# Attention maxima tiles, stack loads and the change of halves in a fused attention and feed-forward kernel

## Chip, cores and metric

One Trainium2 chip, one of its cores. The metric is device time in microseconds (us) of one execution, the median of several runs; less is better. The kernel before takes 1902.88 us (median of 3 runs, 1902.23 to 1906.19).

The engines of a core are named as in the profile: PE (matmul) with PEld (its weight loads), DVE (vector), ACT (scalar), POOL (GpSimd) and SP, which here issues every DMA. SPq, ACTq, POOLq and DVEq are the sequencers of these engines.

## What is computed

2048 tokens of 576 numbers, in float32. The output is a gated mix of an attention with memory over four quarters of 512 tokens (32 heads of 18) and of a feed-forward part of width 4608:

```
g = sigmoid((x * gate_w).sum(-1))
for each quarter s:                       # q, k, v = x @ wq, x @ wk, x @ wv, by heads
    a_dot = softmax(q k^T * scale + mask) v
    a_mem = phi(q) M / (phi(q) z + 1e-6)
    o     = sig(beta) * a_mem + (1 - sig(beta)) * a_dot
    M, z  = M + phi(k)^T v, z + sum phi(k)
a = concat(o) @ wo
b = (silu(x @ w_gate) * (x @ w_up)) @ w_down
out = g * a + (1 - g) * b
```

## The kernel before

**Numbers in parts.** Float32 products are made of high and low parts (`split`, L106: ACT makes the high part, DVE subtracts it). Attention's q and k are kept as three bf16 parts in DRAM (`stk`, "the stacks"), v likewise in `vd`.

**First part, projections** (to about 223 us): for each quarter nine chains of q and k products (`qk`, L301), then eight v steps n = 0 to 7 (`v_step`, L327) with the memory's output (`mem_step`, L397), which writes tiles `om` that SP stores to `med` in the order of the list `late`. In the last quarter the v steps also hold the first weight splits (`w_make`, L215), memsets of the `kst` tiles (L557) and the loads of the first two attention units' stacks (L559).

**Second part, feed-forward and attention together** (about 223 to 1780 us): two halves of the tokens (quarters 2 and 3, then 0 and 1), each with 36 tiles f of the feed-forward width. A tile f has seven product groups (`seven`, L921) from seven combinations of x (`XO`) and seven operands of weights: in the first half made from raw weights and stored to `wc` and `rc` (`keep`, L240), in the second half fetched from there (`w_fetch`, L586). Operand buffers number six. After each group comes a tick (k = 0 to 7, L958), whose `beat` (L866) runs what `defer` has put down for this tick, then at every third f also down groups (`down_group`, L768, PE L778, added up by DVE L783), and steps of attention by a credit. `defer(o + 1, fn)` puts fn on tick o from now. Instructions stand on each engine in the order in which this code emits them.

**Attention** runs in 64 units u of two heads, five steps n = 0 to 4 each (`att_gen`, L709, step number tau = 5u + n). A step makes score blocks for the row maxima (`s_bank`, L608: PE L615, then DVE L622, which writes a scrap tile `scr` and a column of `mb`), and twelve steps later the score blocks again with the maxima as rows added (`t_bank`, L649: PE L655, exponential on ACT L659, mask on POOL L667). After step n = 1, `m_tr` (L626) turns a unit's maxima, which go through DRAM (`mxd`) into rows of the stack tile (`row_load`, L186). The tiles `mb`, two of them, are allocated and set to zero at L604 and L605, after the pools of the first part are closed. The exponentials are split in two (DVE L732, POOL L734) and multiplied with v (L684, L686). Four stack tiles `qst` and `kst` take turns; `stack_load` (L171) loads one unit in ten DMAs, six for the first head and what both share, four for the second; in `att_gen` at L719 unit u + 1 is loaded at steps n = 2 and 3 of unit u. The score blocks of the first head are made at n = 0, those of the second at n = 1.

**Change of halves.** In the last tile of the first half (f = 35) `x_second` (L885) puts down the work on the new x: per z = 0, 1 four raw loads (L892), four sums on POOL (L897), four splits (ACT L107, DVE L108), three loads of kept operands `xd` (L906), and two of `xsd`. After f = 35 come ten beats (`BREAK`, L1018) with the last sixteen down groups, two in a beat from the third beat on.

**DMA order.** All DMAs are issued by SP in the order of the code. They use eight semaphores in turn, and in the built program each waits until the DMA eight before it has landed.

**Last part** (1780 us on): output product, gate and stores.

The functions that the diff touches, and what calls them:

Of the kernel before, what the change touches and what calls it, by code (L numbers as in the profile page):

```python
# [12 lines left out]
F32 = mybir.dt.float32  # L13
# [7 lines left out]
P = 128  # L21
# [3 lines left out]
DH = 18  # L25
L = 512
NSEG = 4
FT = 36
# [8 lines left out]
NB = 8 * NSEG  # L37
# [9 lines left out]
BREAK = 10  # L47
SLOT = (0, 3, 2, 1, 4, 6, 5)
KR = 6 * DH
# [7 lines left out]
def gated_mix(ctx, tc, xT, wf, wd, wv, wo, beta, cmask, ident, bmask, out):  # L57
    nc = tc.nc
# [109 lines left out]
    ast = ExitStack()  # L168
    VP, accs, cur, unit, ms, mts, mbs = {}, {}, {}, {}, {}, {}, []

    def stack_load(u, pr):  # L171
        s, b = divmod(u, 16)
        q, k = (stk[kind, s, 2 * b * DH:2 * b * DH + 2 * DH].rearrange("(j r) z n -> r j z n", r=DH)
                for kind in range(2))
        tq, tk = qst[u % NST], kst[u % NST]
        for z, n in ((0, 3), (1, 2)):
            r0 = (0, 3 * DH)[z]
            qz = q[:, pr, z]
            nc.sync.dma_start(tq[r0:r0 + n * DH, pr],
                              bass.AP(tensor=qz.tensor, offset=qz.offset, ap=[[0, n]] + list(qz.ap)))  # L180
            nc.sync.dma_start(tk[r0:r0 + n * DH, pr], k[:, pr, 0:n].rearrange("r z n -> z r n"))
        if pr == 0:
            nc.sync.dma_start(tq[5 * DH:KR], q[:, :, 2])
            nc.sync.dma_start(tk[5 * DH:KR], k[:, :, 0])

    def row_load(u):  # L186
        nc.sync.dma_start(qst[u % NST][KR:KR + 3].rearrange("z j (i n) -> z (j i) n", n=P), mxd[u])
# [73 lines left out]
    with ExitStack() as st:  # L261
# [228 lines left out]
        for s in range(NSEG):  # L490
# [32 lines left out]
            if s == 3:  # L523
                qst_.close()
                rp = pool(ctx, "rp", 4, side="right")
                wop = pool(ctx, "wop", 6, side="right")
                kq = pool(ast, "kq", 1, side="right")
                for i in range(NST):
                    qst.append(kq.tile([P, 2, L], BF, name=f"qst{i}"))
                    kst.append(kq.tile([P, 2, L], BF, name=f"kst{i}"))  # L530
                for z in range(2):
                    for j, b, kt in ((0, 2, z), (3, 2, 2 + z), (5, 3, 2 + z)):
                        XO[j][z] = xs_of[b][0][kt]
                wraw_of[0] = [w_load(0, u) for u in range(2)]
                start = w_make(0)
            for n in range(8):
                hf, i = divmod(n, 4)
                flush()
                v_step(s, hf, i)
                if s:  # L540
                    mem_step(s, n // 2, n % 2)
                if s < 2 and n > 1 and n - 2 in ((0, 1, 2, 3), (2, 3))[s]:
                    late.append((xd[s, n - 2], f32(xs_of[s][0][n - 2]).rearrange("p a b -> p (a b)")))
                if s < 2 and n == 6:
                    late.append((xsd[s], f32(xs_of[s][1])))
                if s < 3:
                    if n == 0:
                        xs_of[s + 1] = x_tiles(s + 1)
                    if 1 <= n < 6:
                        x_split(xs_of[s + 1], n - 1, raws["x", n - 1])  # L550
                else:
                    if n == 4:
                        wraw_of[1] = [w_load(1, u) for u in range(2)]
                    if n < 2:
                        first_sum(6, n)
                    elif n < 6:
                        nc.gpsimd.memset(kst[n - 2], -1.0)  # L557
                    if n > 3:
                        stack_load(n // 2 - 2, n % 2)  # L559
                    for _ in range((0, 0, 2, 3, 3, 3, 3, 3)[n]):  # L560
                        if start[0][0] < 8:
                            start.pop(0)[1]()
# [7 lines left out]
    with ExitStack() as st:  # L570
# [15 lines left out]
        def w_fetch(f):  # L586
            ops, rem = [None] * 7, [None] * 2
            wops[1, f], wrem[1, f] = ops, rem

            def one(j):  # L590
                ops[j] = op_tile()
                nc.sync.dma_start(f32(ops[j]).rearrange("p a k n -> p (a k n)"), wc[f, j])

            def two(z):
                rem[z] = rem_tile()
                nc.sync.dma_start(f32(rem[z]).rearrange("p a n -> p (a n)"), rc[f, z])

            late = BREAK if f == 0 else 0
            return [(j + 2 + late * (j == 6), lambda j=j: one(j)) for j in range(7)] + [(4, lambda: two(0)), (8, lambda: two(1))]

        kp = pool(ast, "kp", 2, side="right")
        ap = pool(ast, "ap", 2, side="right")
        for i in range(2):
            mbs.append(kp.tile([P, P], F32, name=f"mb{i}", bufs=1))  # L604
            nc.gpsimd.memset(mbs[i], 0.0)  # L605
        SPLAN = [[(0, 0, 3)], [(0, 1, 3)], [(384, 0, 0), (0, 0, 2)], [(384, 1, 0), (0, 1, 2)], [(0, 0, 1), (256, 1, 1)]]

        def s_bank(u, n):  # L608
# [100 lines left out]
        def att_gen():  # L709
            N = 10 * NB  # L710
            for tau in range(N + TL + VL + 4):
# [4 lines left out]
                    nc.sync.dma_start(mxd[u - 1].rearrange("z q n -> q z n"), mts.pop(u - 1))  # L716
                if n == 0 and 2 <= u <= 2 * NB + 1:
                    row_load(u - 2)
                if n in (2, 3) and 0 < u < 2 * NB - 1:  # L719
                    stack_load(u + 1, n - 2)  # L720
                z = tau - TL - VL - 1
                if z % 20 == 0 and 0 <= z < N and z // 20 + 1 < 4 * NSEG:
                    v_fetch(z // 20 + 1)
# [130 lines left out]
        att = att_gen()  # L854
        hs, ds = {}, {}
        seq = [(half, f) for half in range(2) for f in range(FT)]
        v_fetch(0)
        groups = []
        credit = [-1.0]
        yas = {}  # L860
# [24 lines left out]
        def x_second(new, xs):  # L885
# [6 lines left out]
                nc.sync.dma_start(r[z, q], xT[HALF[1][b], :, kt])  # L892

            def total(z, j):
                c, d, e, g = (r[z, q] for q in range(4))
                o, p, q = {1: (c, d, c), 4: (d, g, d), 2: (g, g, c), 6: (e, e, g)}[j]
                nc.gpsimd.tensor_sub(o, p, q)  # L897

# [10 lines left out]
                xs[b] = xs_tile()  # L909
                nc.sync.dma_start(f32(xs[b]), xsd[b])  # L910

            for z, loads, sums, splits in ((0, (0, 1, 5, 4), (6, 6, 7, 7), (8, 8, 9, 10)),
                                           (1, (9, 9, 11, 10), (12, 12, 13, 13), (13, 14, 14, 15))):
                todo += [(o, lambda z=z, q=q: load(z, q)) for o, q in zip(loads, range(4))]
                for o, p, j in zip(sums, splits, (1, 4, 2, 6)):
                    todo += [(o, lambda z=z, j=j: total(z, j)), (p, lambda z=z, j=j: parts(z, j))]
                todo += [(o + z, lambda z=z, j=j: kept(z, j)) for o, j in ((2, 0), (6, 3), (8, 5))]
            todo += [(11 + b, lambda b=b: rest(b)) for b in range(2)]
            return sorted(todo, key=lambda t: t[0])

        def seven(t, w, x, first, last):  # L921
# [15 lines left out]
        for pos, (half, f) in enumerate(seq):  # L937
# [7 lines left out]
            if nxt:  # L945
                plan += w_make(nxt[1]) if nxt[0] == 0 else w_fetch(nxt[1])
                if half == 0 and f + 2 < FT:
                    wraw_of[f + 2] = [None, None]
                    for u in range(2):
                        plan.append(((2, 5)[u], lambda u=u, f=f: wraw_of[f + 2].__setitem__(u, w_load(f + 2, u))))  # L950
            if pos == FT - 1:
                X2, XS2 = [[None, None] for _ in range(7)], [None, None]
                plan += x_second(X2, XS2)
            for o, fn in plan:
                defer(o + 1, fn)
            step = [0]
# [1 line left out]
            def tick():  # L958
# [3 lines left out]
                    while stores:  # L962
                        nc.sync.dma_start(*stores.pop(0))
                if half == 0:
                    if (q, k) in ((0, 0), (1, 3), (2, 1)):
                        draw[f] = d_load(f)
                    if (q, k) in ((1, 0), (1, 7), (2, 5)):
                        g = f - 1 if k == 0 else f
                        ds[half, g] = d_split(g, draw.pop(g))
                elif (q, k) in ((1, 0), (1, 2), (2, 1)):  # L970
                    g = f - 1 if k == 0 else f
                    ds[half, g] = d_fetch(g)
# [141 lines left out]
```

## Time and profile before

| | |
|---|---|
| median of 3 runs | 1902.88 us (1902.23 to 1906.19) |
| the profiled execution | 1903.28 us, of this its span 1901.6 us |
| mean granted PE clock | 0.991 |
| PE busy | 1820.7 us, 96% of the span |
| DVE, ACT, POOL busy | 1217.8, 958.1, 856.6 us |
| DMA | 337.66 MB, mean 178 GB/s, queue busy 53.7% |

How to read the profile: times are us from the start of the span unless marked ns. A row of a group or a timeline has start, duration, engine, line of the kernel, operation, tiles (out<-in) and, in brackets, how long the engine stood idle just before and what ended that. The wait table adds such waits up. The chain of waits is followed back from the last instruction to what released each step; a DMA in it has its time from issue to landing. Tables by stage give the busy time of each engine in a stretch of the span, the granted PE clock (1.00 is full speed) and the share and rate of the DMA engines.

### The profile page before, as it was taken

What the parts mean: (1) busy time and instruction counts of PE and PEld (TensorE: products, weight loads), DVE (VectorE), ACT (ScalarE), POOL (GpSimd) and SP (SyncE); (2) the same over time, 40 slices, a digit from 0 to 9 for tenths busy, and PEclk for the clock granted to TensorE, in tenths of its full rate; (3) what the DMA queues carried; (4) which work ended last, traced back from release to release, by engine and by line L of the source; (5) the groups of instructions that cost most, each with busy time, mean ns of one, the idle gap of its engine ahead of it and who ended that gap; (6) DMA issues with size and microseconds to landing.
All of it is one profiled execution on the core that took longest, in us unless ns stands there. A gap on an engine that the chain in (4) does not pass through costs nothing.

```text
span 1901.6 us, 36530 instructions
## 1 busy us (share of the span) xinstructions
PE 1820.7 (96%) x12508; PEld 1543.4 (81%) x12508; DVE 1217.8 (64%) x3026; ACT 958.1 (50%) x1778; POOL 856.6 (45%) x1246
## 2 busy tenths in 40 slices
PE   8999979999999999999997999999999999999999
PEld 7889857877877887887786788788878878888899
DVE  5555656777777777777775656565565656655455
ACT  7666444466456546645653544543543454354311
POOL 3324522555545555564555445454444444444121
PEclk9999989999999999999998999999999999999999
DMA  6544384466466456645657644654554464445544
GB/s 236 195 170 167 140 303 159 157 228 208 129 214 228 152 170 231 208 151 193 215 165 255 211 139 134 198 154 120 174 172 122 140 196 147 133 154 155 190 150 138
DMA packets 206474, 337.66 MB, mean 178 GB/s; under 512 B 38416, under 2 KB 95888, under 8 KB 206288
## 3 DMA queue, kind: packets, MB, share of 16 engines
q1 hardware_dynamic: 206288, 335.32, 53.7%
q8 instruction: 100, 1.64, 0.3%
q14 instruction: 86, 0.70, 0.1%
HBM read 197.48 MB, written 137.76 MB: 176 GB/s over the span
## 4 chain that ended last, share of the span: by engine, by line
PE 76%; DVE 7%; DMA 6%; ACT 5%; issue 3%; SPq 1%; POOL 1%; ACTq 0%; DVEq 0%; POOLq 0%
PE bank L925 25%; PE bank L778 23%; PE bank L130 11%; PE bank L931 5%; PE bank L655 3%; PE bank L615 3%; PE bank L684 2%; DMA raw<-in_wf_dram 1%; PE bank L686 1%; ACT L659 1%; DMA woraw<-in_wo_dram 1%; DMA draw<-in_wd_dram 1%; PE bank L362 1%; ACT hh L107 1%; ACT pe L659 1%
## 5 line engine op out<-in xcount | busy, mean ns | idle before, releaser
L734 POOL TENSOR_TENSOR p<-pe,p 128x512 f16<-128x512 f32 x320 | 374.4, 1170 | 684.7 <-DVE p L732 595.1
L778 PE MATMUL bank<-dw,hh 128*128 128x288 f32 x2304 | 482.7, 302 | 21.4 <-DVE ya L783 9.7
L778 PEld LDWEIGHTS bank<-dw,hh 128*128 128x128 f32 x2304 | 379.4, 189 | 43.7 <-DVE ya L783 17.0
L659 ACT ACTIVATE pe<-bank 128x512 f32<-128x512 f32 x320 | 191.2, 598 | 346.0 <-PE bank L655 285.4
L778 PE MATMUL bank<-dw,hl 128*128 128x288 f32 x1152 | 341.1, 296 | 2.0 <-DVE hl L108 2.0
L783 DVE TENSOR_TENSOR ya<-bank,ya 128x288 f32<-128x288 f32 x352 | 160.2, 456 | 232.7 <-PE bank L778 230.7
L622 DVE CUSTOM_DVE_ANT_0 scr<-bank,cm 128x512 bf16<-128x512 f32 (+3 forms) x512 | 247.2, 483 | 15.9 <-PE bank L615 9.1
L778 PEld LDWEIGHTS bank<-dw,hl 128*128 128x128 f32 x1152 | 217.6, 189 | 2.6 <-DVE hl L108 2.6
L655 PE MATMUL bank<-qst,kst 111*128 111x512 bf16 (+3 forms) x512 | 151.7, 305 | 0.7 <-DMA qst<-mxd 0.7
L732 DVE CAST p<-pe 128x512 f16<-128x512 f32 x320 | 150.8, 472 | 0.3 <-POOL pe L667 0.3
L667 POOL TENSOR_SCALAR_AFFINE_SELECT pe<-pe 128x256 f32<-128x256 f32 (+1 forms) x320 | 135.4, 423 | 14.0 <-ACT pe L659 12.8
L615 PE MATMUL bank<-kst,qst 108*128 108x512 bf16 (+3 forms) x512 | 126.3, 300 | 13.2 <-ACT pe L659 12.2
L1006 DVE TENSOR_TENSOR bank<-bank,row 128x512 f32<-128x512 f32 x72 | 50.3, 699 | 110.3 <-ACT row L1002 109.7
L659 ACT ACT_TABLE_LOAD x66 | 84.7, 1283 | 49.2 <-PE bank L655 48.2
L993 ACT ACTIVATE row<-bank 128x512 f32<-128x512 f32 x72 | 43.1, 598 | 127.4 <-PE bank L931 127.0
L108 DVE TENSOR_TENSOR hl<-row,hh 128x512 fp32r<-128x512 f32 x72 | 51.9, 721 | 85.6 <-ACT hh L107 85.6
L130 PE MATMUL bank<-xo,qhi 128*128 128x512 f32 x288 | 92.8, 403 | 5.1 <-ACT xo L107 5.0
L655 PEld LDWEIGHTS <-kst 111*128 111x128 bf16 x512 | 47.9, 97 | 52.3 <-issue 36.9
L997 ACT ACTIVATE bank<-bank 128x512 f32<-128x512 f32 x72 | 41.9, 582 | 90.7 <-PE bank L925 86.8
L999 ACT ACT_TABLE_LOAD x67 | 86.0, 1283 | 1.2
L318 POOL TENSOR_TENSOR q<-qr,q 128x512 bf16<-128x512 f32 x36 | 43.8, 1217 | 93.6 <-ACT q L317 86.9
L982 ACT ACTIVATE bank<-bank 128x512 f32<-128x512 f32 x72 | 42.0, 583 | 82.0 <-PE bank L925 72.0
(2085 smaller groups left out, 4238.1 us busy)
## 6 DMA issues: line engine op xcount, KB each, us to landing
raw<-in_wf_dram SPq DMA_DIRECT2D x72, 320.0 KB
dc<-dw SPq DMA_DIRECT2D x36, 576.0 KB
dw<-dc SPq DMA_DIRECT2D x36, 576.0 KB
stk<-q SPq DMA_DIRECT2D x32, 384.0 KB
draw<-in_wd_dram SPq DMA_DIRECT2D x36, 288.0 KB
vd<-vps SPq DMA_DIRECT2D x8, 912.0 KB
v<-vd SPq DMA_DIRECT2D x16, 456.0 KB
qst<-stk SPq DMA_DIRECT2D x128, 54.0 KB
```

Source lines behind the costliest of these rows:

```text
L130: nc.tensor.matmul(t, st[n], mv[n], start=(n == 0), stop=(n == 13))
L615: nc.tensor.matmul(t[:, c:c + w], qs[:KR, pr, P * i:P * i + P], ks[:KR, pr, 0:w], start=True, stop=True)
L622: nc.vector.tensor_tensor_reduce(scr[:, :w], t[:, c:c + w], cm[:, L - w:L], 1.0, -3.0e38, OP.add, OP.max, m[:, k:k + 1])
L655: nc.tensor.matmul(t[:, c:c + w], ks[:KR + 3, pr, P * j:P * j + P], qs[:KR + 3, pr, P * j:L], start=True, stop=True)
L659: nc.scalar.activation(pe, t, AF.Exp, scale=SCALE)
L667: nc.gpsimd.affine_select(d, d, pattern=pat, compare_op=OP.is_ge, fill=0.0, base=0, channel_multiplier=-1)
L732: nc.vector.tensor_copy(p1, pe)
L734: nc.gpsimd.tensor_sub(p2, pe, p1)
L778: nc.tensor.matmul(t, p, q[:, cs], start=(n == 0), stop=(n == 3 * CH - 1))
L783: nc.vector.tensor_add(ya[:, i, cs], t, ya[:, i, cs])
L925: nc.tensor.matmul(t, w[:, p, z], x[z][:, q], start=first and n == 0, stop=last and n == 5, skip_group_check=True)
L931: nc.tensor.matmul(t, w[:, p], xs, start=False, stop=p == 1, skip_group_check=True)
```

## The change

- `mb` is allocated with the stack tiles and set to zero by POOL in the v steps n = 6 and 7 of the last quarter. What was allocated behind it in `kp` (`scr` and others) moves to its place.
- `stack_load` becomes `stack_loads`, a list of the same ten DMAs. In the v steps only unit 0 is loaded, two DMAs a step from n = 3 on. In `att_gen` unit u + 1 is loaded from u = 0 on in three, three and four DMAs at steps n = 2, 3 and 4.
- The first load of v, `v_fetch(0)`, is put down for the sixth beat.
- `x_second` is put down one tile earlier with 8 more ticks, so that ticks may be negative: the first two raw loads go to ticks -3 and -2 of f = 35, sums, splits, kept operands and `xsd` to other ticks.
- `w_fetch(0)` of the second half: operands 0 to 5 five ticks later, the remainders six; operand 6 stays.
- In the first half `d_load` of every third f moves from k = 0 to k = 3.

```diff
--- before.py
+++ after.py
@@ -168,20 +168,22 @@
     ast = ExitStack()
     VP, accs, cur, unit, ms, mts, mbs = {}, {}, {}, {}, {}, {}, []
 
-    def stack_load(u, pr):
+    def stack_loads(u):
         s, b = divmod(u, 16)
         q, k = (stk[kind, s, 2 * b * DH:2 * b * DH + 2 * DH].rearrange("(j r) z n -> r j z n", r=DH)
                 for kind in range(2))
         tq, tk = qst[u % NST], kst[u % NST]
-        for z, n in ((0, 3), (1, 2)):
-            r0 = (0, 3 * DH)[z]
-            qz = q[:, pr, z]
-            nc.sync.dma_start(tq[r0:r0 + n * DH, pr],
-                              bass.AP(tensor=qz.tensor, offset=qz.offset, ap=[[0, n]] + list(qz.ap)))
-            nc.sync.dma_start(tk[r0:r0 + n * DH, pr], k[:, pr, 0:n].rearrange("r z n -> z r n"))
-        if pr == 0:
-            nc.sync.dma_start(tq[5 * DH:KR], q[:, :, 2])
-            nc.sync.dma_start(tk[5 * DH:KR], k[:, :, 0])
+        r = []
+        for pr in range(2):
+            for z, n in ((0, 3), (1, 2)):
+                r0 = (0, 3 * DH)[z]
+                qz = q[:, pr, z]
+                r += [(tq[r0:r0 + n * DH, pr],
+                       bass.AP(tensor=qz.tensor, offset=qz.offset, ap=[[0, n]] + list(qz.ap))),
+                      (tk[r0:r0 + n * DH, pr], k[:, pr, 0:n].rearrange("r z n -> z r n"))]
+            if pr == 0:
+                r += [(tq[5 * DH:KR], q[:, :, 2]), (tk[5 * DH:KR], k[:, :, 0])]
+        return r
 
     def row_load(u):
         nc.sync.dma_start(qst[u % NST][KR:KR + 3].rearrange("z j (i n) -> z (j i) n", n=P), mxd[u])
@@ -528,6 +530,8 @@
                 for i in range(NST):
                     qst.append(kq.tile([P, 2, L], BF, name=f"qst{i}"))
                     kst.append(kq.tile([P, 2, L], BF, name=f"kst{i}"))
+                for i in range(2):
+                    mbs.append(kq.tile([P, P], F32, name=f"mb{i}"))
                 for z in range(2):
                     for j, b, kt in ((0, 2, z), (3, 2, 2 + z), (5, 3, 2 + z)):
                         XO[j][z] = xs_of[b][0][kt]
@@ -555,8 +559,11 @@
                         first_sum(6, n)
                     elif n < 6:
                         nc.gpsimd.memset(kst[n - 2], -1.0)
-                    if n > 3:
-                        stack_load(n // 2 - 2, n % 2)
+                    else:
+                        nc.gpsimd.memset(mbs[n - 6], 0.0)
+                    if n > 2:
+                        for z in stack_loads(0)[2 * n - 6:2 * n - 4]:
+                            nc.sync.dma_start(*z)
                     for _ in range((0, 0, 2, 3, 3, 3, 3, 3)[n]):
                         if start[0][0] < 8:
                             start.pop(0)[1]()
@@ -595,14 +602,11 @@
                 rem[z] = rem_tile()
                 nc.sync.dma_start(f32(rem[z]).rearrange("p a n -> p (a n)"), rc[f, z])
 
-            late = BREAK if f == 0 else 0
-            return [(j + 2 + late * (j == 6), lambda j=j: one(j)) for j in range(7)] + [(4, lambda: two(0)), (8, lambda: two(1))]
+            late = [5 * (1 + (j == 6)) * (f == 0) for j in range(7)]
+            return [(j + 2 + late[j], lambda j=j: one(j)) for j in range(7)] + [(4 + 6 * (f == 0) + 4 * z, lambda z=z: two(z)) for z in range(2)]
 
         kp = pool(ast, "kp", 2, side="right")
         ap = pool(ast, "ap", 2, side="right")
-        for i in range(2):
-            mbs.append(kp.tile([P, P], F32, name=f"mb{i}", bufs=1))
-            nc.gpsimd.memset(mbs[i], 0.0)
         SPLAN = [[(0, 0, 3)], [(0, 1, 3)], [(384, 0, 0), (0, 0, 2)], [(384, 1, 0), (0, 1, 2)], [(0, 0, 1), (256, 1, 1)]]
 
         def s_bank(u, n):
@@ -716,8 +720,9 @@
                     nc.sync.dma_start(mxd[u - 1].rearrange("z q n -> q z n"), mts.pop(u - 1))
                 if n == 0 and 2 <= u <= 2 * NB + 1:
                     row_load(u - 2)
-                if n in (2, 3) and 0 < u < 2 * NB - 1:
-                    stack_load(u + 1, n - 2)
+                if n > 1 and u + 1 < 2 * NB:
+                    for d in stack_loads(u + 1)[(0, 3, 6)[n - 2]:(3, 6, 10)[n - 2]]:
+                        nc.sync.dma_start(*d)
                 z = tau - TL - VL - 1
                 if z % 20 == 0 and 0 <= z < N and z // 20 + 1 < 4 * NSEG:
                     v_fetch(z // 20 + 1)
@@ -854,7 +859,7 @@
         att = att_gen()
         hs, ds = {}, {}
         seq = [(half, f) for half in range(2) for f in range(FT)]
-        v_fetch(0)
+        defer(6, lambda: v_fetch(0))
         groups = []
         credit = [-1.0]
         yas = {}
@@ -892,7 +897,7 @@
                 nc.sync.dma_start(r[z, q], xT[HALF[1][b], :, kt])
 
             def total(z, j):
-                c, d, e, g = (r[z, q] for q in range(4))
+                c, d, e, g = (r.get((z, q)) for q in range(4))
                 o, p, q = {1: (c, d, c), 4: (d, g, d), 2: (g, g, c), 6: (e, e, g)}[j]
                 nc.gpsimd.tensor_sub(o, p, q)
 
@@ -909,13 +914,13 @@
                 xs[b] = xs_tile()
                 nc.sync.dma_start(f32(xs[b]), xsd[b])
 
-            for z, loads, sums, splits in ((0, (0, 1, 5, 4), (6, 6, 7, 7), (8, 8, 9, 10)),
-                                           (1, (9, 9, 11, 10), (12, 12, 13, 13), (13, 14, 14, 15))):
+            for z, loads, sums, splits in ((0, (-3, -2, 5, 4), (4, 7, 8, 8), (5, 9, 9, 10)),
+                                           (1, (9, 10, 12, 11), (13, 13, 14, 14), (14, 15, 15, 16))):
                 todo += [(o, lambda z=z, q=q: load(z, q)) for o, q in zip(loads, range(4))]
                 for o, p, j in zip(sums, splits, (1, 4, 2, 6)):
                     todo += [(o, lambda z=z, j=j: total(z, j)), (p, lambda z=z, j=j: parts(z, j))]
-                todo += [(o + z, lambda z=z, j=j: kept(z, j)) for o, j in ((2, 0), (6, 3), (8, 5))]
-            todo += [(11 + b, lambda b=b: rest(b)) for b in range(2)]
+                todo += [(o + z, lambda z=z, j=j: kept(z, j)) for o, j in ((6, 0), (12, 3), (14, 5))]
+            todo += [(16 + b, lambda b=b: rest(b)) for b in range(2)]
             return sorted(todo, key=lambda t: t[0])
 
         def seven(t, w, x, first, last):
@@ -948,9 +953,9 @@
                     wraw_of[f + 2] = [None, None]
                     for u in range(2):
                         plan.append(((2, 5)[u], lambda u=u, f=f: wraw_of[f + 2].__setitem__(u, w_load(f + 2, u))))
-            if pos == FT - 1:
+            if pos == FT - 2:
                 X2, XS2 = [[None, None] for _ in range(7)], [None, None]
-                plan += x_second(X2, XS2)
+                plan += [(o + 8, fn) for o, fn in x_second(X2, XS2)]
             for o, fn in plan:
                 defer(o + 1, fn)
             step = [0]
@@ -962,7 +967,7 @@
                     while stores:
                         nc.sync.dma_start(*stores.pop(0))
                 if half == 0:
-                    if (q, k) in ((0, 0), (1, 3), (2, 1)):
+                    if (q, k) in ((0, 3), (1, 3), (2, 1)):
                         draw[f] = d_load(f)
                     if (q, k) in ((1, 0), (1, 7), (2, 5)):
                         g = f - 1 if k == 0 else f
```

## Prediction

> **What bounds the kernel now.** First the engine shares of the page: TensorE (PE) is busy for 1820.7 of 1901.6 us, 96%; vector, scalar and GpSimd engines 64%, 50%, 45%. So only about 81 us can be won, where PE stands still, and some more where its granted clock is low. Next the table by stages (busy us of PE, PEld, DVE, ACT, POOL; then granted clock, DMA share, GB/s):
>
> ```profile
> 223.00:276.00 53.00, 38.66 (x162) 29.74 (x161) 28.68 (x68) 26.82 (x63) 12.41 (x18) 0.87 0.70 251
> 276.00:1004.00 728.00, 697.70 (x4746) 580.99 (x4745) 541.11 (x1328) 413.39 (x815) 364.38 (x529) 1.00 0.57 191
> 1004.00:1043.00 39.00, 28.27 (x204) 25.87 (x204) 24.84 (x54) 8.76 (x17) 23.10 (x25) 0.78 0.69 256
> 1043.00:1780.00 737.00, 725.19 (x5338) 604.06 (x5337) 433.11 (x1156) 344.87 (x553) 345.41 (x542) 1.00 0.50 154
> ```
>
> The two short stages hold 25 of the 81 us idle, and are the only ones of these with a clock under 1.00: the change from projections to feed-forward, and the change of halves. The diff works at both. Third, the timelines of the first, engine by engine:
>
> ```profile
> 236.80 0.61 PE L931 MATMUL bank<-xs,wr__2586 128*128 128x512 f32 x2
> 249.88 2.93 PE L925 MATMUL bank<-xo,wo__2616 128*128 128x512 f32 x6 [12.47 <-DVE bank L1006]
> ...
> 246.25 0.42 ACT L228 ACTIVATE wo__2627<-ws 128x256 fp32r<-128x256 f32 x1 [11.46 <-POOL ws L224]
> ...
> 245.18 0.35 POOL L605 MEMSET mb<- 128x128 f32 x2 [18.44 <-DMA med<-om]
> ```
>
> Read backwards: PE waits for L1006, this for L1002 on ACT, which stands in order behind L228, whose sum L224 stands on POOL behind the memset of L605. That one waits for the last store of `om`, which had its memory before. In the chain of waits (start, us) that store takes 6.49 us, and an earlier stack load 5.25:
>
> ```profile
> 232.54 5.25 DMA kst<-stk
> 238.30 6.49 DMA med<-om
> ```
>
> The change of halves, timelines again, and the chain for the load at its root:
>
> ```profile
> 1013.01 0.85 PE L778 MATMUL bank<-dw,hh 128*128 128x288 f32 x2 [7.38 <-ACT hh L107]
> ...
> 1011.81 0.63 ACT L107 ACTIVATE xo<-raw 128x512 fp32r<-128x512 f32 x1 [7.09 <-POOL raw L897]
> ...
> 1010.51 4.28 POOL L897 TENSOR_TENSOR raw<-raw 128x512 f32<-128x512 f32 x3 [7.89 <-DMA raw<-in_xT_dram]
> 1004.41 5.97 DMA raw<-in_xT_dram
> ```
>
> The first down group needs hh; its split stands on ACT behind a split of x, this behind POOL's sums, these behind the third raw x load, issued at 1004.41.
>
> **Part 1, maxima and first loads.** The memsets (0.18 us each) move into the v steps n = 6 and 7 and wait for nothing there; POOL has 18.44 us idle right after. Ten of twenty stack loads (unit 1's) leave SP's queue there. Counting SP's rows from 221.80, the last `om` store now has 13 issues ahead, about 7.0 us by their rows (0.61 to 0.75 for 54 and 36 rows, 0.30 to 0.45 for others), and some waits for the DMA eight before: issue at 229.5 instead of 238.30.
>
> What is late next is ACT's own chain, by its rows: L997 ends at 234.8, L228 takes 0.4, table and Silu (L999) 1.8, L1002 0.55, then L1006 0.70: 238.25. PE is ready at 237.41. So f = 1 starts at 238.25, not 249.88: **11.6 us**. L228 needs the store of an operand buffer: issued at 227.05 by the same count, 4.6 us in flight, 231.7, before ACT is there (234.8). The clock is the second gain: the three first products of f = 1 took 6.2 us, at full clock 4.2 (1.36 each by the rows of f = 2 and a score block): **2.0 us**. A new wait: `scr` now lies on the memory that `om` leaves, and the first L622 on DVE waits for the last `om` store; behind it would stand L989 and PE. Landing 229.5 + 6.5 = 236.0; L622 ran 7 us after f = 1 began, so it comes at 242 or later: hidden, cover 6 us. Without cover it costs what the landing lacks, at most the old 11.6. v_fetch(0), six ticks later, takes its wait for the stores out of SP's way (6.1 us in the wait table); v is first read 19 steps of attention later. Sum 13.6 us; bounds 6 (the stage's DMA, at 327 to 405 GB/s after 250, holds the operands up by half) and 15.
>
> **Part 2, the change of halves.** Two raw x loads go three ticks earlier (into f = 34), and the kept operands and the first weight fetches go behind the third and fourth. Before, eight DMAs (two of 512 KB) were issued between 999.30 and 1004.41 ahead of the third. By SP's rows in the new order: the `dc` and `atd` stores, four stack loads (moved here from 985.6), two `wc`, one `rc`, then the third raw at about 1001.3, with 4.9 us in flight 1006.2 instead of 1010.38. POOL's sums are no longer in one piece: 1.3, then L734 1.17 and L667 0.86 between, then 1.3; the ACT splits of x that follow end at 1011.4, `hh`'s second half at 1012.0, the exponential 1012.6. The first half of hh is free of them (1005.6), but PE's second down group stands behind a score block that needs that exponential's bank, and behind the row load, for which I count 1011.6 (before 1016.62). So PE idles from about 1007 to 1012.8 and starts its second group there instead of 1017.21: **4.4 us**. I take 4.5. Bounds: 2 (one more SP wait eats half) and 15 (no stall left, which the rows would allow only if the row load and the exponential were 5 us earlier). The later fetches have their cover: operands 0 to 5 are asked for by tick 12 and `xs` by tick 17, f = 0 begins at 18 and reads `xs` at 21; eight beats of 2.4 us of groups lie between.
>
> The clock decides what is left of a stall's price:
>
> ```profile
> 238.00:240.00 2.00, 0.00 (x0) 0.00 (x0) 0.00 (x0) 0.00 (x0) 0.00 (x0) 0.97 0.76 306
> 240.00:242.00 2.00, 0.00 (x0) 0.00 (x0) 0.00 (x0) 0.00 (x0) 0.00 (x0) 0.50 0.86 334
> ...
> 1006.00:1008.00 2.00, 0.00 (x0) 0.00 (x0) 0.00 (x0) 0.00 (x0) 0.00 (x0) 0.97 1.03 407
> 1008.00:1010.00 2.00, 0.00 (x0) 0.00 (x0) 0.00 (x0) 0.00 (x0) 0.00 (x0) 0.50 1.06 396
> ```
>
> 0.97 over a slice of 2 us is one in which 0.12 us ran at 0.50, so the clock fell at 239.9 and 1007.9, about 2.5 and 2.3 us after PE's last matmul. My remaining gap of 5.8 us at the change of halves is longer, so a slow stretch follows it as before (1013.0 to 1024.5, with three waits inside, against 249.9 to about 253 at the first change); I leave it its length, since DVE's additions (L783) still stand behind splits of x and keep PE waiting inside it.
>
> The Trainium skill (TensorE: Matmul & The Clock Gate, section What's actually happening) says that about 3.4 us of sustained work bring the clock back. The first change agrees with some 3.3 us, the second does not, with 11.5 us in all. By that rule the stretch would be up to 5 us shorter if the waits inside go, a gain of half of that, and the time 1885 instead of 1887.
>
> **Part 3, stack loads by twos, threes and fours.** For each later unit nothing is saved in number; six and four DMAs at steps 2 and 3 become three, three and four at 2, 3, 4. The four of the second head now come one step later and are needed two steps on. One unit of the second half:
>
> ```profile
> 1329.51 0.73 SPq L179 DMA_DIRECT2D qst<-stk  x1
> ...
> 1332.38 0.61 SPq L181 DMA_DIRECT2D kst<-stk  x1
> ...
> 1335.41 0.42 SPq L714 DMA_DIRECT2D atd<-ob  x1
> ...
> 1339.94 0.38 PE L615 MATMUL bank<-kst,qst 108*128 108x512 bf16 x1
> ```
>
> Last load 1332.38, landing about 4.1 to 5.3 later (1337.7 by the trace's semaphore updates), use 1339.94: 2.3 us in hand. New place: behind the `atd` store. If the DMAs ahead keep their times, the four start at 1335.9, the last at 1338.0, landing 1342.1: 2.2 us late. If they move up by the four that left (3.0 us), it lands at 1339.1, in time. I did this for all units with 4.1 us in flight. Rigid: 17 come late on the second head and 2 on the first, 18.8 us together. Moving up where SP's rows stand back to back: 6 late, 5.7 us. Gains on the other side: PE's three waits for `wc` fetches in the second half, 2.8 us together, and `d_load` at k = 3 no longer holds SP for the previous split (25.4 us in ten waits, all off PE's path, so nothing). Between +3 and -18.8 I take **-2**, near the row that moves up less the small gain.
>
> **Sum.** 13.6 + 4.5 - 2 = 16.1 us. The profiled execution took 1903.28 (span 1901.6 and 1.7 around it), 0.4 above the median of the runs shown (1902.88): 1903.28 - 16.1 = **1887 us**.
>
> **The rivals.**
> A. Stack loads too late: half to most of the rigid count is paid (10 to 18 us) and 0 to 8 of the gain is left: 1895 to 1903. For it: hands of 2 to 4 us in a dozen units of the second half. Against: fewer DMAs stand in a bunch, and flight times of 2.8 to 3 also occur.
> B. The wait at the first change only moves: to L622 on DVE or to operand buffers whose stores crowd one another; 6 of 13.6 us come: 1895. For it 405 GB/s there; against, the counted covers of 3 and 6 us.
> C. The change of halves opens fully: 10 us more, 1877. For it the raw loads ahead; against, the row load and POOL's split order.
> D. Slower: the second head's loads also miss in the first half, where SP waits for splits, and each miss of over 2.3 us drops the clock and costs some 2 us more. It decides when flight under load is 5.2 us, as in the chain row, for all: rigidly counted 48.7 us late, against 18 won: 1934 at worst, 1910 if half.
> That the change does not do what it says would be B with nothing won at the first change: 1901.
>
> **How the numbers follow.** Forecast (1881 to 1892) 0.62, A 0.14, B 0.07, C 0.10, D 0.07. The range 1876 to 1899 takes in C and most of A and B and leaves out D and the rest of A. Under 0.2% (3.8 us, about what a measurement of this kernel can tell from no change) counts as same: faster 0.86, same 0.08, slower 0.06.
>
> **What would show it.** Right: no memset wait on POOL, PE's gap before the second feed-forward tile under 2 us, clock 1.00 there; a third raw load landing some 4 us earlier, a PE gap of 4 to 6 us left at the change of halves; a few L615 waits for kst or qst, under 6 us together. Wrong: a DVE wait of L622 for `med`, L615 waits above 10 us, or a gap at the halves as long as before.

## The result and the profile after

The changed kernel takes **1898.39 us** (median of 20 runs, 1892.71 to 1906.59), the kernel before 1902.97 (20 runs): a ratio of 0.9971, 95% interval 0.9961 to 0.9981. The forecast was 1887. By the ratio 5.5 us were won (4.6 by the medians), not 16.

The table by stages, with the same columns and cuts as for the kernel before (busy us of PE, PEld, DVE, ACT, POOL; granted clock, DMA share, GB/s):

```profile
223.00:276.00 53.00, 50.40 (x239) 40.19 (x238) 39.37 (x93) 30.97 (x73) 15.28 (x19) 1.00 0.85 302
276.00:1004.00 728.00, 691.21 (x4687) 576.37 (x4687) 537.74 (x1314) 413.81 (x815) 368.65 (x534) 0.99 0.57 191
1004.00:1043.00 39.00, 37.83 (x295) 32.95 (x295) 25.73 (x64) 12.00 (x20) 21.98 (x31) 0.97 0.75 245
1043.00:1780.00 737.00, 716.14 (x5263) 597.62 (x5262) 427.03 (x1137) 338.32 (x543) 337.24 (x532) 1.00 0.49 151
```

Both short stages are nearly full, at a clock near 1.00 (before: 38.66 of 53 and 28.27 of 39). But the two long ones have become emptier: 36.8 and 20.9 us idle, before 30.3 and 11.8. The cuts are fixed in time, and the work has moved under them (the change of halves now lies at 996 to 1006), so I also compare the start of the n-th matmul of PE, after minus before. PE runs the same 12508 matmuls in nearly the same order. The drift also strays where no code differs: up to f = 34 the run of part 2 alone goes between -1.2 and 1.4, and the run of the memset alone goes from 1.2 to 5.9 between 280 and 970 us. There the clock fell four times for 3.41 us at a time, in the kernel before once, and half speed for 3.41 us costs 1.7.

| matmul, time after | drift, us | with the stack loads back |
|---|---|---|
| 1200, 212 us (before the first change) | -0.9 | -0.7 |
| 2000, 360 | -13.7 | -12.5 (matmul 2400) |
| 6000, 962 (before the change of halves) | -11.3 | -12.0 |
| 6400, 1032 | -15.3 | -17.4 (matmul 6600) |
| 8800, 1368 | -9.3 | -17.6 (matmul 9000) |
| 10800, 1649 | -5.4 | -16.5 |

So 12.8 us were won at the first change, 4.0 at the change of halves, and 2.4 and 9.9 lost again along attention; the 2.4 are within what the drift strays by. The wait table of PE names who took them (total us, times, longest):

```profile
PE bank L619 <- DMA kst<-stk: 11.6, 11, 2.1
...
PE bank L659 <- DMA qst<-mxd: 7.6, 3, 6.5
...
PE bank L619 <- DMA wc<-wo__11212: 3.4, 1, 3.4
...
PE bank L619 <- DMA wo__20455<-wc: 1.8, 1, 1.8
```

No row of before names a stack load. L619 reads only stacks, so the two rows with operands are misnamed: the first of these waits ended at 864.9, where by the trace's semaphore updates unit 24's last stack load landed (864.8), while the store it names landed at 867.06. That makes 13 waits and 16.8 us. From the last landing of a head's loads to its first matmul there were at least 2.1 us in every case before. Now 20 of 128 heads have under 0.7, and the median of the second heads in the second half fell from 4.80 to 2.04.

### The profile page after: what moved, and what is told of

Its sections match the earlier page's. It is cut to its first block, busy times and chain, and to the rows that moved or that the text cites. A ratio compares the mean times of both kernels' runs of the same rounds, so it can differ in the third digit from the quotient of the medians.

```text
span 1896.5 us, 36496 instructions
## 1 busy us (share of the span) xinstructions
PE 1820.1 (96%) x12508; PEld 1544.5 (81%) x12508; DVE 1217.4 (64%) x3026; ACT 958.4 (51%) x1778; POOL 854.6 (45%) x1246
## 4 chain that ended last, share of the span: by engine, by line
PE 70%; DMA 10%; DVE 7%; ACT 5%; issue 3%; SPq 3%; POOL 1%; DVEq 0%; ACTq 0%; POOLq 0%
PE bank L783 23%; PE bank L930 21%; PE bank L130 11%; PE bank L936 4%; PE bank L619 3%; PE bank L659 3%; DMA kst<-stk 2%; SPq L725 2%; PE bank L688 2%; DMA raw<-in_wf_dram 1%; PE bank L690 1%; DMA qst<-stk 1%; DMA qst<-mxd 1%; ACT L663 1%; DMA woraw<-in_wo_dram 1%
## 5 line engine op out<-in xcount | busy, mean ns | idle before, releaser
L783 PE MATMUL bank<-dw,hh 128*128 128x288 f32 x2304 | 482.1, 302 | 11.4 <-DVE ya L788 7.4
L626 DVE CUSTOM_DVE_ANT_0 scr<-bank,cm 128x512 bf16<-128x512 f32 (+3 forms) x512 | 247.4, 483 | 23.3 <-PE bank L619 16.5
L619 PE MATMUL bank<-kst,qst 108*128 108x512 bf16 (+3 forms) x512 | 126.4, 300 | 28.5 <-DMA kst<-stk 11.6
L671 POOL TENSOR_SCALAR_AFFINE_SELECT pe<-pe 128x256 f32<-128x256 f32 (+1 forms) x320 | 134.5, 420 | 15.2 <-ACT pe L663 12.5
L619 PEld LDWEIGHTS <-qst 108*128 108x128 bf16 x512 | 50.3, 99 | 54.5 <-issue 34.1
L1002 ACT ACTIVATE bank<-bank 128x512 f32<-128x512 f32 x72 | 41.9, 582 | 91.3 <-PE bank L930 87.8
```

What stands on the lines that cost most here:

```text
L619: nc.tensor.matmul(t[:, c:c + w], qs[:KR, pr, P * i:P * i + P], ks[:KR, pr, 0:w], start=True, stop=True)
L626: nc.vector.tensor_tensor_reduce(scr[:, :w], t[:, c:c + w], cm[:, L - w:L], 1.0, -3.0e38, OP.add, OP.max, m[:, k:k + 1])
L671: nc.gpsimd.affine_select(d, d, pattern=pat, compare_op=OP.is_ge, fill=0.0, base=0, channel_multiplier=-1)
L783: nc.tensor.matmul(t, p, q[:, cs], start=(n == 0), stop=(n == 3 * CH - 1))
```

## Experiments

**Undo the stack loads, or do them alone.** The first run is the changed kernel with

```diff
-                if n > 1 and u + 1 < 2 * NB:
-                    for d in stack_loads(u + 1)[(0, 3, 6)[n - 2]:(3, 6, 10)[n - 2]]:
+                if n in (2, 3) and u + 1 < 2 * NB:
+                    for d in stack_loads(u + 1)[(0, 6)[n - 2]:(6, 10)[n - 2]]:
```

> The changed kernel with one thing undone: the stack loads of each unit go out again as six at step n = 2 and four at n = 3, in place of three, three and four at 2, 3 and 4. Unit 1's loads stay out of the v steps. Theory L (the second head's four loads come a step too late; in the changed kernel's trace 20 of 128 heads have under 0.7 us between the last landing and the first matmul, against none before, and PE lies 12 us further back at the end of attention than after the two gains): the whole loss of some 11 to 12 us goes, 1898.4 becomes 1887 (1884 to 1890), PE's waits of L619 for kst or qst loads fall from 11.6 us to under 3, and the drift against the kernel before stays between -15 and -18 us from 1050 to the end. Rival O (the loss comes from the other moves, d_load at k = 3, the later first v load, or from DMA contention that the earlier start of everything brings): the time stays at 1896 to 1900 and other DMA waits take the place.

Measured: 1887.22 us, ratio to before 0.9911 (0.9898 to 0.9923). No row of L619 for a stack load is left in PE's wait table, and the drift stays at -16 to -18 from 1058 on (right column above). The stage that had lost most, in the same columns:

```profile
1043.00:1780.00 737.00, 724.70 (x5301) 604.39 (x5300) 430.96 (x1147) 341.96 (x551) 340.10 (x532) 1.00 0.50 156
```

The second run is the kernel before with the loads by threes and fours from unit 2 on, unit 1 staying in the v steps (`stack_loads` as in the change):

```diff
-                if n in (2, 3) and 0 < u < 2 * NB - 1:
-                    stack_load(u + 1, n - 2)
+                if n > 1 and 0 < u and u + 1 < 2 * NB:
+                    for d in stack_loads(u + 1)[(0, 3, 6)[n - 2]:(3, 6, 10)[n - 2]]:
+                        nc.sync.dma_start(*d)
```

> The kernel before with the stack loads of units 2 to 63 by three, three and four at n = 2, 3, 4, and nothing else. Theory L: slower by 10 to 14 us, 1912 to 1917, with 15 or more heads whose loads land under 0.7 us before use. Rival O: within 3 us of 1903.

Measured: 1915.66 us, ratio 1.0062 (1.0048 to 1.0076), 11.8 us slower; 18 heads under 0.7 us. Theory L stands, by both. This kernel also shows what a long miss costs, in PE's timeline and in slices of 2 us:

```profile
1484.51 0.59 PE L618 MATMUL bank<-kst,qst 108*128 108x512 bf16 x1 [3.43 <-DMA wo__19665<-wc]
```
```profile
1482.00:1484.00 2.00, 0.00 (x0) 0.00 (x0) 0.00 (x0) 0.00 (x0) 1.37 (x2) 0.87 0.85 310
1484.00:1486.00 2.00, 1.49 (x5) 1.15 (x6) 0.70 (x2) 0.57 (x2) 0.00 (x0) 0.50 0.14 55
...
1488.00:1490.00 2.00, 2.00 (x6) 1.54 (x5) 0.00 (x0) 1.80 (x2) 0.08 (x1) 0.50 0.41 108
1490.00:1492.00 2.00, 2.00 (x9) 1.64 (x8) 0.32 (x1) 1.29 (x3) 0.00 (x0) 0.93 0.22 46
```

The load had 6.89 us in flight (issued 1477.49, landed 1484.38, a 576 KB `dw` right behind it). PE stood 3.43 us, the clock was at 0.50 from 1483.47 to 1490.30, and the drift grew by 6.3 us there, nearly twice the wait: 3.43 us, and half of the 5.79 us that PE worked at half speed.

**How the loads are divided.** Two more divisions, of the changed kernel: three at n = 2 and seven at n = 3; and six, two and two.

```diff
-                if n > 1 and u + 1 < 2 * NB:
-                    for d in stack_loads(u + 1)[(0, 3, 6)[n - 2]:(3, 6, 10)[n - 2]]:
+                if n in (2, 3) and u + 1 < 2 * NB:
+                    for d in stack_loads(u + 1)[(0, 3)[n - 2]:(3, 10)[n - 2]]:
```
```diff
-                    for d in stack_loads(u + 1)[(0, 3, 6)[n - 2]:(3, 6, 10)[n - 2]]:
+                    for d in stack_loads(u + 1)[(0, 6, 8)[n - 2]:(6, 8, 10)[n - 2]]:
```

> The changed kernel with a unit's stack loads as three at step 2 and seven at step 3, none at step 4. Theory P (what counts is the step in which the last load of a head goes out: a step is some 3 us of the second half, a queue of three more loads some 2): the second head's last load goes out some 2 us earlier than in the changed kernel and up to 1 us later than with six and four, so its median slack in the second half is 4 to 5 us against 2.04 and 4.82, few heads are late, and the time is 1887 to 1890. Rival Q (a bunch of seven on SP's queue is as bad as the later step, because at most eight DMAs are outstanding): slack under 3 us and 1892 to 1898.

> The changed kernel with a unit's stack loads as six at step 2, two at step 3 and two at step 4. Theory P: although two of the second head's four go out earlier, the last two stand at step 4, so the slack is only one or two issue times (0.6 to 1.2 us) better than in the changed kernel: median 2.5 to 3.5 us, half or more of the 11 us loss stays, 1892 to 1898. Rival Q: the bunches are smaller, and most of the loss goes, 1887 to 1890.

Measured: 1892.67 (0.9932, 0.9917 to 0.9947) and 1890.27 (0.9924, 0.9910 to 0.9937). Neither theory holds. P gave the slack: median 4.26 and 3.24 us for the second heads of the second half. It did not give the times; those came near to Q's, whose slack (under 3 us with seven) did not come. With six, two, two, 12 second heads come with under 0.7 us, but PE waits at most 6.7 us for them (4.2 us under the name of a stack load, 2.5 at such matmuls under other names), and the time is near the best. With seven at once the stacks are in time (0.8 us of waits), yet the time is some 5 us worse than with six and four (the first run): waits for operand fetches (6.4 us in six, with six and four 2.9 in four) and for hh (1.7, 1.5, there 0.7) have grown. Its profiled execution was the slowest of its five, and in it the clock fell six times for 3.41 us, in that of six and four once; the intervals of the three divisions touch. So how these 5 us divide stays open. A count of late heads is no price.

**The first change, alone and in its pieces.** Part 1 alone is the kernel before with the memsets moved as in the change and with SP's queue relieved:

```diff
-                    if n > 3:
-                        stack_load(n // 2 - 2, n % 2)
+                    if n > 2:
+                        for z in stack_loads(0)[2 * n - 6:2 * n - 4]:
+                            nc.sync.dma_start(*z)
...
-                if n in (2, 3) and 0 < u < 2 * NB - 1:
-                    stack_load(u + 1, n - 2)
+                if n in (2, 3) and u + 1 < 2 * NB:
+                    for d in stack_loads(u + 1)[(0, 6)[n - 2]:(6, 10)[n - 2]]:
+                        nc.sync.dma_start(*d)
...
-        v_fetch(0)
+        defer(6, lambda: v_fetch(0))
```

Part 2 alone has the change's hunks in `w_fetch` and `x_second` and this one:

```diff
-            if pos == FT - 1:
+            if pos == FT - 2:
...
-                plan += x_second(X2, XS2)
+                plan += [(o + 8, fn) for o, fn in x_second(X2, XS2)]
```

> The kernel before with part 1 alone: the maxima's tiles beside the stacks with their memsets in the last two v steps, unit 1's stack loads at unit 0's steps 2 and 3 (six and four), unit 0's by twos from n = 3, the first v load six ticks later. If part 1 stands by itself, as the drift at matmul 1800 of the changed kernel says (-13 to -13.7 us): 1889 to 1891. If it needs the others or is given back at the change of halves (where PE waits for a load at a time set by SP and not by PE): 1894 to 1900.

> The kernel before with part 2 alone: the raw x loads, kept operands, and first weight fetches of the second half in the changed order. The changed kernel's trace shows a drift of -4.1 us across the change of halves, with a 6.5 us wait for a row load that took 7.56 us and no wait for hh. If that is the part's own worth: 1898 to 1900. If the row load is late only because the stack loads stand ahead of it in the changed kernel (three of them between 985 and 990), the wait is shorter here and the time 1893 to 1896. If the part gives nothing alone: 1903.

Measured: 1895.34 (0.9953, 0.9940 to 0.9966) and 1898.83 (0.9969, 0.9958 to 0.9980). Part 2 is worth what was forecast by itself. Part 1 is 3 to 4 us short, and not at the change of halves: right after the first change (252 to 262 us) the drift is -10.7, in the first run -14.4. SP's wait table and ACT's timeline of part 1 alone say why:

```profile
SPq L205 <- DMA vd<-vps: 5.5, 1, 5.5
```
```profile
239.52 0.42 ACT L230 ACTIVATE wo__2633<-ws 128x256 fp32r<-128x256 f32 x1 [3.13 <-DMA wc<-wo__2467]
```

The load of the first down weight (L205) is here still at k = 0. It waits on SP for the store whose memory it takes, and behind it stand the operand stores that free ACT's buffers. So the moves were taken one by one. The memset alone is the kernel before with

```diff
+                for i in range(2):
+                    mbs.append(kq.tile([P, P], F32, name=f"mb{i}"))
...
+                    else:
+                        nc.gpsimd.memset(mbs[n - 6], 0.0)
...
-        for i in range(2):
-            mbs.append(kp.tile([P, P], F32, name=f"mb{i}", bufs=1))
-            nc.gpsimd.memset(mbs[i], 0.0)
```

The queue alone is the diff of part 1 above without that. The best kernel (the first run) was run with this memset edit undone, and with the load of the down weight put back; the last run is the kernel before with the latter's reverse alone.

```diff
-                    if (q, k) in ((0, 3), (1, 3), (2, 1)):
+                    if (q, k) in ((0, 0), (1, 3), (2, 1)):
```

> The kernel before with the maxima's tiles and memsets moved as in the changed kernel, and the queue of SP left as it was. Theory S (SP's queue holds the end of the stage, the memset only shows it first): POOL and ACT are free at 234 to 238, and the second feed-forward tile starts near 238 instead of 249.9, but its third group needs the operand buffer whose store was issued at 246.25 before, behind the last store of om and the first v load; PE waits there till 250 or so, and 2 to 4 us are won: 1900 to 1902. Rival M (the memset's wait is the cause, as the prediction's reading back from PE took it): 8 to 12 us are won, 1892 to 1896.

> The kernel before with SP's queue relieved as in the run of part 1 alone (unit 1's stack loads later, unit 0's by twos, first v load six ticks later), the memsets left where they were. Theory S: the memset still waits, but for a store that goes out at 229.7 and lands at 236 to 236.5; the tile starts at 241 instead of 249.9 and then waits less than part 1 alone did at its third group: 1895 to 1898, nearly as much as part 1 alone (1895.3). Rival M: at most a third of part 1's gain, 1901 or more.

> The changed kernel with the stack loads back (as in the first run) and also the load of the first down weight back at step 0 of its tile. In the run of part 1 alone, which has it there, SP stands 5.5 us at this load, waiting for a store of vd that has its memory, and four stores of operands behind it go out at 236 to 237.5 instead of 229.7 to 232.8; ACT waits 3.13 us for one of them. If that is what part 1 alone lacked (its drift at the change of phase was -10.8, with the load at step 3 it was -14.1): 1890 to 1892, against 1887.2. If the prediction was right to price this move at nothing: 1886 to 1888.

> The fastest version so far (the changed kernel with the stack loads back as six and four, 1887.2) with the maxima's tiles and memsets put back where the kernel before has them; SP's queue and the load of the down weight stay as changed. The memset alone was worth nothing (1.0007) and the queue alone as much as both (0.9958 against 0.9953), but both runs had the down weight's load in front of the operands' stores. Theory C (three waits cover one another; with the other two gone the memset's own wait comes to the path): the memset runs at 237 to 238 as in the run of the queue alone, the second feed-forward tile starts at 241 to 242.5 instead of 236.5 to 237, and 4 to 6 us are lost, some of it as slow clock: 1891 to 1894. Rival N (the move of the memset is worth nothing in any company): 1886 to 1888.5.

> The kernel before with the load of the first down weight of each three at step 3 instead of step 0, and nothing else. It was worth 4 to 5 us in company of the others (1892.1 against 1887.2). Theory C: the first v load stands in front of it on SP, waits for the same stores, and the memset waits besides, so nothing is won alone: within 2 us of the kernel before. Rival: it gives its 3 to 5 us by itself, 1899 to 1901.

| run | ratio to before |
|---|---|
| memset alone | 1.0007 (0.9997 to 1.0018) |
| down weight at k = 3 alone | 1.0011 (0.9999 to 1.0022) |
| queue alone | 0.9958 (0.9944 to 0.9971) |
| queue and memset (part 1 alone) | 0.9953 (0.9940 to 0.9966) |
| best kernel, memset put back | 0.9943 (0.9930 to 0.9957) |
| best kernel, down weight back at k = 0 | 0.9935 (0.9918 to 0.9952) |
| best kernel | 0.9911 (0.9898 to 0.9923) |

The memset alone only cuts one gap into two, in PE's timeline of that run, with the store that holds the second in SP's:

```profile
242.31 2.93 PE L926 MATMUL bank<-xo,wo__2616 128*128 128x512 f32 x6 [4.42 <-DVE bank L1007]
252.46 2.90 PE L926 MATMUL bank<-xo,wo__2627 128*128 128x512 f32 x6 [7.22 <-DVE row L1011]
```
```profile
246.13 0.42 SPq L241 DMA_DIRECT2D wc<-wo__2475  x1
```

4.42 and 7.22 are 11.64 us, against the one gap of 12.47 before. In the best kernel with the memset back, POOL runs it at 235.98 and PE's gap is there again:

```profile
235.98 0.34 POOL L608 MEMSET mb<- 128x128 f32 x2 [9.92 <-DMA wc<-wo__2557]
```
```profile
240.68 2.06 PE L929 MATMUL bank<-xo,wo__2604 128*128 128x512 f32 x6 [4.27 <-DVE bank L1010]
```

The POOL row names another store; by the chain of waits it was the last store of `om`, landed at 235.53.

Three waits covered one another, as theory C had it. The queue's is the longest, and its relief gives 8 us alone. Once it is gone, the memset and the down weight are each the last with the other out of the way: 4.4 and 4.9 us (1891.64 and 1892.14 against 1887.22; the interval of the latter touches that of the best kernel). Alone both give nothing.

**The row load at the change of halves.** In the best kernel, the first two kept operands three beats later:

```diff
-for o, j in ((6, 0), (12, 3), (14, 5))]
+for o, j in ((9, 0), (12, 3), (14, 5))]
```

> The changed kernel with the stack loads back and the first two kept operands (512 KB each) asked for three beats later at the change of halves. They were issued ahead of the row load that PE waits for (2.46 us with the stack loads back, 6.51 in the changed kernel; issued 992.64, used 998.5). If the row load is late because they share its DMA engines (about 1 MB at 290 to 400 GB/s, 2.5 to 3.6 us): the wait goes, and with it some of the slow clock behind it, 1883 to 1886. If PE then waits as long for the splits of x or for the exponential's bank (their waits of 1.0 to 1.5 us stand beside it): 1886 to 1888.

Measured: 1888.83 (0.9918, 0.9902 to 0.9934), no gain. The row load's wait is gone (2.46 us), and PE stands at the next matmul:

```profile
1001.83 0.59 PE L619 MATMUL bank<-kst,qst 108*128 108x128 bf16 x2 [2.96 <-ACT pe L663]
```

That is the exponential behind the splits of x on ACT, as the second case had it. By the semaphore updates the row load took 2.96 us from issue to landing here, with the two 512 KB loads issued behind it, and 5.86 us in the best kernel, with them ahead. So they do hold it up; that this is by shared DMA engines fits, but is not shown.

## Why the prediction was wrong

**Part 1, right in size.** The second tile was to start at 238.25; it starts at 237.00, its memsets long done:

```profile
237.00 1.65 PE L930 MATMUL bank<-xo,wo__2604 128*128 128x512 f32 x6
```
```profile
226.07 0.20 POOL L563 MEMSET mb<- 128x128 f32 x1
```

13.6 us were forecast, the drift says 12.8. The clock stays at 1.00, and DVE's first maximum comes at 242.71 without a wait for `med`. One reason in it was wrong: the move of `d_load` "so nothing". It is worth some 3 to 5 us (3.1 by the drift right after the first change, 4.9 by the medians), and the sum held it all the same, since it counted the stores' times without SP's wait at that load. Nor does the memset deserve its place in the reading back from PE: it was the first of three waits, and alone worth nothing.

**Part 2, right.** 4.5 us forecast; 4.0 by the drift, 5.4 with the stack loads back, 5.9 alone (0.9969). Counted in the time of before (PE is 11.3 us ahead), the third raw load goes out at 1002.0 (forecast 1001.3), and the gap ends at 1013.9 (1012.8) with the row load, which the forecast had among the two last. This row load took longer than counted:

```profile
995.03 7.56 DMA qst<-mxd
```

**Part 3 is the step that failed: "Between +3 and -18.8 I take -2, near the row that moves up less the small gain."** It was -11.4 (0.9971 against 0.9911) or -11.8 (alone). The rigid count had 19 late heads and 18.8 us; measured were 20 heads and 16.8 us of waits, of which 11 to 12 stayed at the end. The moving-up count had six heads and 5.7 us. The unit shown in the prediction, in SP's and PE's timelines of the changed kernel:

```profile
1325.14 0.61 SPq L725 DMA_DIRECT2D kst<-stk  x1
```
```profile
1329.91 0.38 PE L619 MATMUL bank<-kst,qst 108*128 108x512 bf16 x1 [1.50 <-DMA kst<-stk]
```

Until 1326.5 PE is 10.73 us ahead of before. In the time of before, the load goes out at 1335.9 (moving up: 1335.0; rigid: 1338.0), lands 4.52 us later at 1340.4 (forecast 1339.1, with 4.1 in flight), and PE is ready not at 1339.94 but at 1339.0: its wait of 0.71 us before, which ended at 1338.35, is gone (the row there names ACT; the operand fetch that it reads had landed at 1338.22, and now stands ahead of the four loads). Three small things took a reserve of 0.8 us. SP's rows ahead closed up only in part, since they are no queue of ready work: SP stood 0.44, 0.74, 1.01 and 0.35 us ahead of the four rows in front of these loads, for a buffer or for the DMA eight before. (Its fetches L599 wait 133.4 us in 70 waits for PE's L930 between 1045 and 1700.) Over the second half the last issue of a second head lies 6.99 us ahead of use against 9.89 (medians), so 2.9 us were lost. In the ten units there in which PE waited, the loads went out 0.2 to 2.3 us ahead of the rigid count (median 1.1); the moving-up count had 3.0 at the unit shown.

That alone does not make the loss. With the issue times that the changed kernel has, and the flight of 4.1 us that the prediction took for every load, the heads would be late by little (flight is the time from issue to landing):

| issue times | in flight | heads late | us late |
|---|---|---|---|
| prediction, moving up | 4.1 | 6 | 5.7 |
| prediction, rigid | 4.1 | 19 | 18.8 |
| trace of the changed kernel | 4.1 | 10 | 6.6 |
| trace of the changed kernel | as measured | 14 | 15.3 |

So the term that was mis-sized most is the flight: 4.1 us is near the median over all heads in the kernel before (4.16), but the second heads' last loads, the ones that were moved, took 4.53 there (one in ten 5.3 or more; the unit shown 5.27), and 4.45 after. The longest late one took 6.84. That the rigid count comes so near to the measured waits is luck, of two errors: with the measured flights it gives 29 us in the second half alone, where the heads were 8.0 us late. This is a recount from the traces; no run changed the flight alone.

Rival A (10 to 18 us paid, 1895 to 1903) was what happened, and had 0.14. Its evidence was on the table, reserves of 2 to 4 us in a dozen units, against a cost of one step.

The Trainium skill (TensorE: Matmul & The Clock Gate, section What's actually happening) lets some 3.4 us of sustained work bring the clock back, counted in a window of that length that runs freely. The trace agrees: after the 3.43 us miss above PE worked 5.8 us without a gap (1484.5 to 1490.3) before the clock rose, since the slow stretch was two windows long (6.83 us), and the first still held 1.04 us of the miss. The slow stretch that the prediction holds against this rule is no exception either: its windows held 3.41, 2.57, 1.32 and 0.53 us in which PE stood, and the first without any was the last. Nor is 2.3 us of wait the limit, as rival D had it: a wait of 2.07 us (461.31 in the changed kernel) lowered the clock, one of 2.30 us (877.33 in the kernel before) did not.

## What to carry to other kernels

A load that is moved one step later on a shared in-order queue can lose most of that step, where rows ahead of it wait for the consumer: in the ten units above 3.8 of 4.9 us (medians). Count the reserve of every instance, and count it with the flight times of just these loads and their spread: one median for all loads more than halved the loss here. Where a stall has several waits in parallel, the one that the chain names may be worth nothing alone. Ask of each what is late next, and test them in company.

## What the hardware showed

- A wait of 3.43 us cost 6.3 us: the clock stood at 0.50 from 2.4 us after the last matmul until 5.8 us after the next.
- In all 14 traces the granted clock changes only on a grid of 3.41 us, whose place differs from run to run. Between 225 and 1780 us it fell only after a step of the grid in which PE had stood 1.40 us or more (by its matmul rows), and always from 1.92 us on; it rose after every slow step with at most 0.42 us of standing, and after none with 0.53 or more. So one and the same wait costs differently: PE's wait of 2.07 us ahead of matmul 2646 brought a slow stretch in the changed kernel (463.41 to 466.83) and none in the kernel before.
- A DMA of few bytes is held up by large ones issued ahead of it: the row load of 3 by 1024 elements took 7.56 us behind two 512 KB loads and a 576 KB store, 5.86 us in the best kernel, and 2.96 us with the two loads issued after it.
- The last stack load of a second head, 36 rows, took 4.5 us in the median from issue to landing, and up to 7.04 (in the kernel before with threes and fours).
- The name of the DMA that ends a wait can be that of a later one: two of PE's waits for stacks carry the names of weights.
